# Loading and converting the first layer's weights later in an mLSTM + Fourier-mix kernel

## The chip, the cores and the metric

The kernel runs on one core of one Trainium2 chip. The metric is the device time of one execution in microseconds; lower is better. The time before is the median of six runs.

## The reference

The work is two layers, one behind the other. The first is an mLSTM cell over 4 batches, 8 heads, 768 steps and a head size of 40:

```python
m_new = max(f_t + m, i_t);  fs = exp(f_t + m - m_new);  is_ = exp(i_t - m_new)
C = fs * C + is_ * outer(v_t, k_t);  n = fs * n + is_ * k_t
y_t = sigmoid(o_t) * (C @ q_t) / max(abs(n . q_t), 1)
```

Its output, seen as (4, 768, 320), is x of the second layer, a Fourier mix with an MLP (320 to 1280 to 320):

```python
u = x + real(fft(fft(x, axis=1), axis=2))
un = (u - mean(u)) / sqrt(var(u) + 1e-6)
out = u + relu(un @ w_ch1) @ w_ch2
```

The weights of the MLP come to the kernel as 64-bit floats. The kernel itself makes 32-bit floats of them.

## The kernel before

**Slots.** Every step of the work is a small function, entered into a plan with `at(slot, phase, fn)`. `run` then calls the functions in the order of slot and phase (`EVAC` 0, `FILL` 1, `MAIN` 2, `FILL_PE` 3, with fractions between), and the instructions of each engine stand in that order in its queue. A slot is no fixed time. What decides is the order alone: an engine takes its instructions one by one, and each waits by semaphores for what it needs. All loads are issued by SyncE (SP), in the order of the plan too.

**The first batch.** Batch 0 goes through the mLSTM in six chunks of 128 steps, one every three slots from slot 0 on. For a chunk, ScalarE (ACT) makes the exponentials W (`mlstm_exp`, L491), TensorE (PE) the scores (`mlstm_scores`, L539), VectorE (DVE) weighs them (`mlstm_weigh`, L545), PE makes the products from the state and the chunk (L553, L560, L570, L575), ACT copies the new state and heads out (`mlstm_gather`, L583 to L601), PE turns the heads (`mlstm_turn`, L611), and DVE divides and gates (`mlstm_finish`, L712 to L720). GpSimd (POOL) scales values and states (L507, L530, L501). The Fourier mix of batch 0 folds pairs of chunks at slots 16, 19 and 22 (`mix_fold`, L812 to L830, DVE and POOL), multiplies with the tables (`mix_seq`, `mix_tail`, L901 to L904), adds and takes statistics (`mix_add`, L955 to L963), centres (`mix_center`, uc, L971), turns (L978) and copies out (L983). `halves_of_chunks` (L342, L347 on POOL, among others) prepares the other batches beside it.

**The MLP.** Its first products of batch 0 (`mlp_in`, L1056, and L1047 for the 64 middle features) begin at slot 31, one f of ten for the first half of the tokens in each slot; `mlp_relu` (L1071, ACT) follows. From slot 32 on, the mLSTM of batch 1 runs between them in half chunks (`halves_...`, L515, L519, L652, L667, L672), with a copy of one element on ACT (`halves_between`, "warm", L699) between two groups of PE products.

**The weights.** They come in ten pieces of 128 x 640 numbers, `Piece` (L382): five of w_ch1, then five of w_ch2. Counted from 0, pieces 0 and 3 of w_ch1 are the first and the second half of the columns of rows 0 to 127, pieces 1 and 4 the same of the last 128 rows, and piece 2 is the 64 rows between (`w1t_sb`). A piece has four steps: `load` (L396, 640 KB, SP), `take` (two DVE operations: exponent e, L406, and upper mantissa m, L408), `convert` (two ACT operations, L413 and L414) and `join` (three DVE operations, L420, L422 and L426; the last writes the weights). Two `raw` buffers take turns, so the load of piece n waits until piece n - 2 is joined; of e and m there is one buffer each.

Product f of `mlp_in` uses the second half of the columns (pieces 3 and 4) from f = 4 and f = 5 on, at slots 35 and 36; piece 2 is first used at f = 1.

Of the kernel before, what the change touches and what calls it, by code (L numbers as in the profile page):

```python
# [53 lines left out]
def kernel(  # L54
# [87 lines left out]
    def gates(gp):  # L142
# [40 lines left out]
        w1_pieces[0].load()  # L183
        nc.sync.dma_start(out=spread_sb, in_=spread)
        mlstm_load(0, 2)
        w1_pieces[1].load()
        for t in hT_bufs + Cd_bufs + [h_first]:
            nc.gpsimd.memset(t, 0.0)

# [192 lines left out]
    class Piece:  # L382
# [33 lines left out]
        def join(self):  # L416
# [7 lines left out]
            for d in self.dst:  # L424
# [5 lines left out]
    w1_pieces = [Piece([w1_sb[:, f // 2, f % 2 * part:(f % 2 + 1) * part]], w_ch1[:, f * part:(f + 1) * part])  # L430
                 for f in (0, 2, 1, 3)]
# [16 lines left out]
    def mlstm_load(b, c):  # L448
        k = chunks[b, c] = Chunk()
        i = b * NT + c  # L450
        k.qk = qk_bufs[i % NQ]
        k.C = [C_bufs[(i + n) % 3] if b == 0 else states[(b * NS + 2 * c + n) % len(states)] for n in range(3)]
        for hip in range(2):
            nc.sync.dma_start(out=k.qk[hip * 64:hip * 64 + D], in_=qkT[b, c, hip])
        kvt = kvp.tile([L, H * (D + D1) + LH - D], FP, name="kvt", tag="kvt")
        nc.sync.dma_start(out=kvt, in_=kv[b, c])
        k.v, k.k = kvt, kvt[:, H * D1:]
        k.v1 = k.v[:, 0:H * D1].rearrange("p (h d) -> p h d", d=D1)
        k.kn = k.k[:, 0:H * D].rearrange("p (h d) -> p h d", d=D)
# [844 lines left out]
    ctx.enter_context(tc.manual_schedule())  # L1304
    gates_pool = ExitStack()
    gates(gates_pool.enter_context(tc.tile_pool(name="gates", bufs=1)))


# [31 lines left out]

    at(60, FILL + 0.4, lambda: nc.gpsimd.memset(ds_sb[0:1, 0, 0, :], 1.0))

    when = [((2, 0.7), (4, 0.5), (6, 0.6)), ((6, 0.7), (7, 0.5), (8, 0.6)), ((11, 0.7), (13, 0.5), (22, 0.6))]
    when += [((22, 0.7), (23, 0.7), (31, 0.5)), ((31, 0.7), (32, 0.7), (33, 0.6))]
    when += [((s, 0.7), (s + 1, 0.7), (s + 2, 0.6)) for s in (36, 39, 42, 48, 51)]
    pieces = w1_pieces + w2_pieces
    for n, (w, p) in enumerate(zip(when, pieces)):
        if n > 4:
            at(when[n - 2][2][0] + 1, FILL + 0.7, p.load)
        for (s, phase), fn in zip(w, (p.take, p.convert, p.join)):  # L1350
            at(s, FILL + phase, fn)

    early = [(3, mlstm_load, 3), (3, mlstm_load_o, 2), (4, mlstm_load, 4), (5, mlstm_load_decay, 3),
             (5, mlstm_load_decay, 4), (6, None, 2), (7, mlstm_load_o, 3), (7, mlstm_load, 5),
             (11, mlstm_load_decay, 5), (11, None, 3), (11, mlstm_load_o, 4), (12, load_tables, None),
             (14, mlstm_load_o, 5), (23, None, 4)]
    for s, load, c in early:
        at(s, FILL + 0.8, *((pieces[c].load,) if load is None else (load,) if c is None else (load, 0, c)))

# [127 lines left out]
```

## Time and profile before

| | us |
|---|---|
| median of 6 runs | 396.47 |
| lowest, highest | 395.22, 396.68 |
| time of the profiled execution | 396.68 |
| its span, first to last instruction | 395.0 |

| stretch, us | what runs | DVE busy | ACT busy | POOL busy | DMA engines busy |
|---|---|---|---|---|---|
| 10 to 15 | first chunks of batch 0 | 3.49 | 3.96 | 4.53 | 1.03 |
| 25 to 30 | chunks | 4.61 | 4.39 | 2.79 | 0.94 |
| 40 to 45 | last chunk, first folds | 4.66 | 3.00 | 2.34 | 0.47 |
| 50 to 55 | mix of batch 0 | 4.13 | 2.90 | 0.00 | 1.02 |
| 65 to 70 | first MLP products, batch 1 begins | 3.52 | 3.71 | 3.41 | 1.05 |
| 75 to 80 | the same | 4.66 | 2.72 | 1.16 | 0.55 |

Busy times are microseconds out of the five of each stretch; the share of the DMA engines is 1 when all 16 are busy. The granted clock of TensorE is 1.00 throughout. The slots can be read in the trace from their operations: the first load of a piece is issued at 4.54 us, the takes of the ten pieces start at 14.1, 22.3, 31.5, 52.3, 61.9, 79.0, 86.8, 94.6, 109.0 and 117.1 us, and the first MLP product starts at 59.55 us.

In lines of the timeline, the columns are the start (us from the start of the span), the busy time (us), the engine, the source line, the operation, the tile written and those read, shapes and count; a bracket holds the idle time of the engine before it and what ended that. Lines of the chain of waits have the start, the time and what the chain ran through.

### The profile page before, as it was taken

To read this page: it belongs to the slowest core of one execution; us is meant where nothing else is said; L and a number is where in the kernel's file an instruction comes from. 1 tells how busy PE (TensorE), PEld (TensorE's weight loads), DVE (VectorE), ACT (ScalarE), POOL (GpSimd) and SP (SyncE) were. 2 spreads that over 40 slices of the span, in tenths; PEclk is the share of its full clock that TensorE was granted. 3 is DMA by queue.
4 is the path that set the end of the run, shared out by engine and by line. 5 is a ranking of instruction groups with operands and counts; after the bars stand their busy time and mean duration, and the time that the engine had idled before them with its cause. 6 is when DMAs were issued, how large, how long until landed. Compare 5 with 4: busy or idle time off the path is not lost.

```text
span 395.0 us, 10580 instructions
## 1 busy us (share of the span) xinstructions
PE 380.1 (96%) x4174; PEld 277.1 (70%) x4174; DVE 278.6 (71%) x671; ACT 172.1 (44%) x481; POOL 134.5 (34%) x237
## 2 busy tenths in 40 slices
PE   8999899999999999998999989989999899999996
PEld 6878555556566677664579978755588896556996
DVE  7789988599599677566975598767655785336652
ACT  6887357477443124653462314554530123454000
POOL 5749514377944423271354133541400000020000
PEclk9999999999999999999999999999999999999999
DMA  7988499667692445539400627400000010000000
GB/s 213 295 232 224 153 239 246 193 206 224 190 233 73 145 97 157 147 87 223 121 15 32 157 56 198 146 20 2 0 2 33 0 36 33 2 0 0 35 33 35
DMA packets 25631, 44.78 MB, mean 113 GB/s; under 512 B 5727, under 2 KB 14766, under 8 KB 25454
## 3 DMA queue, kind: packets, MB, share of 16 engines
q1 hardware_dynamic: 25582, 44.11, 40.2%
q8 instruction: 33, 0.54, 0.6%
q14 instruction: 16, 0.13, 0.1%
HBM read 38.49 MB, written 4.12 MB: 108 GB/s over the span
## 4 chain that ended last, share of the span: by engine, by line
PE 75%; DVE 16%; issue 3%; ACT 3%; DMA 1%; POOL 1%; SPq 0%; DVEq 0%; ACTq 0%; POOLq 0%
PE po L1237 18%; PE pm L1118 14%; PE po L1181 8%; PE pm L1056 6%; PE ph L519 4%; PE pm L1123 3%; PE pu L935 3%; PE ps L519 3%; PE pm L1047 2%; PE put L978 2%; PE pz L904 1%; PE pz L892 1%; DVE so L716 1%; DVE h L1127 1%; DVE x L1187 1%
## 5 line engine op out<-in xcount | busy, mean ns | idle before, releaser
L1187 DVE SCALAR_TENSOR_TENSOR x<-po,rstd,x 128x160 f32<-128x160 f32 (+1 forms) x69 | 26.9, 394 | 40.9 <-PE po L1237 36.8
L1127 DVE TENSOR_TENSOR h<-h,pm 128x384 f32<-128x384 f32 x60 | 30.5, 549 | 29.0 <-PE pm L1123 13.8
L1118 PE MATMUL pm<-uT,w_sb 128*128 128x384 f32 x90 | 37.7, 506 | 2.1 <-DVE h L1127 1.3
L652 POOL TENSOR_TENSOR C<-C,decB 128x164 f32<-128x164 f32 x30 | 15.9, 531 | 69.5 <-DVE C L667 53.0
L491 ACT ACTIVATE W<-W,colT 128x64 f32<-128x64 f32 x144 | 37.5, 339 | 0.0
L1181 PE MATMUL po<-w_sb,h 128*128 128x320 f32 x120 | 34.3, 435 | 0.0
L515 POOL TENSOR_SCALAR_AFFINE_SELECT W<-W 64x512 f32<-64x512 f32 x36 | 27.3, 758 | 12.9 <-ACT W L491 11.4
L1002 POOL TENSOR_TENSOR t<-rstd 128x6 f32<-128x6 f32 x12 | 3.3, 274 | 80.7 <-DVE v L996 80.2
L1237 PE MATMUL po<-T,S 128*128 128x160 f32 x180 | 27.9, 302 | 1.5 <-DVE x L1187 1.5
L1056 PE MATMUL pm<-uT,w_sb 128*128 128x384 f32 x80 | 29.2, 500 | 0.1
L1181 PEld LDWEIGHTS po<-w_sb,h 128*128 128x128 f32 x120 | 22.2, 190 | 9.6 <-issue 0.6
L501 POOL TENSOR_TENSOR qg<-qk,Gb 128x512 f32<-128x512 f32 (+1 forms) x21 | 27.4, 1305 | 1.2 <-DMA Gb<-G_d 1.2
L1237 PEld LDWEIGHTS po<-T,S 128*128 128x128 f32 x180 | 25.5, 190 | 3.2 <-DVE x L1187 2.0
L1118 PEld LDWEIGHTS pm<-uT,w_sb 128*128 128x128 f32 x90 | 15.5, 189 | 16.4 <-DVE h L1127 7.5
L1237 PE MATMUL po<-w_sb,h 128*128 128x160 f32 x180 | 26.3, 300 | 0.0
L1237 PEld LDWEIGHTS po<-w_sb,h 128*128 128x128 f32 x180 | 25.2, 190 | 1.4 <-DVE x L1187 0.3
L1174 ACT ACTIVATE h<-h 128x384 f32<-128x384 f32 x45 | 23.1, 520 | 2.0 <-DVE h L1127 2.0
L507 POOL TENSOR_TENSOR vw<-kvt,colT 128x328 f32<-128x328 f32 x23 | 19.4, 845 | 13.1 <-DMA qk<-in_qkT 10.1
L983 ACT COPY uT<-put 128x384 f32<-128x384 f32 x24 | 11.1, 477 | 29.0 <-PE put L978 29.0
L1123 PE MATMUL pm<-uT,w1t_sb 64*128 64x384 f32 x120 | 23.4, 508 | 0.0
L971 ACT ACTIVATE uc<-x 128x384 f32<-128x384 f32 x24 | 14.4, 613 | 17.9 <-DVE x L963 11.9
L1056 PEld LDWEIGHTS pm<-uT,w_sb 128*128 128x128 f32 x80 | 14.1, 189 | 9.6 <-issue 1.9
(241 smaller groups left out, 843.7 us busy)
## 6 DMA issues: line engine op xcount, KB each, us to landing
kvt<-in_kv SPq DMA_DIRECT2D x24, 336.0 KB
qk<-in_qkT SPq DMA_DIRECT2D x48, 160.0 KB
raw<-in_w SPq DMA_DIRECT2D x10, 640.0 KB
Gb<-G_d SPq DMA_DIRECT2D x36, 128.0 KB
W<-M_d SPq DMA_DIRECT2D x36, 128.0 KB
so<-in_o SPq DMA_DIRECT2D x24, 160.0 KB
out<-x SPq DMA_DIRECT2D x24, 160.0 KB
x<-so SPq DMA_DIRECT2D x9, 140.0 KB
```

The lines of the kernel that those rows point to most:

```text
L491: nc.scalar.activation(out=k.W[:, h, :], in_=M, func=AF.Exp, scale=-1.0, bias=colT[:, c, 0, b * H + h:b * H + h + 1])
L501: nc.gpsimd.tensor_tensor(out=k.qg[:, :, t], in0=k.qk[:, 0, :, t], in1=k.Gb[:, :, t], op=OP.mult)
L515: nc.gpsimd.affine_select(out=W, in_=W, compare_op=OP.is_ge, fill=0.0, base=base, pattern=[[0, H], [step, LH]], channel_multiplier=-1)
L519: nc.tensor.matmul(out, w, x, start=start, stop=True, skip_group_check=True)
L1056: nc.tensor.matmul(k.pm[i], w1_sb[:, ch, f0:f0 + L], u[2 * ch], start=(ch == 0 and not ahead), stop=(ch == 1 and ahead), skip_group_check= ...
L1118: nc.tensor.matmul(bank, w, u, start=start, stop=True, skip_group_check=True)
L1123: nc.tensor.matmul(bank, block(w1t_sb, i)[rows], mlp_u(gr, 1)[rows], start=False, stop=True, skip_group_check=True)
L1127: nc.vector.tensor_tensor(out=h, in0=h, in1=bank, op=OP.add)
L1174: nc.scalar.activation(out=h, in_=h, func=AF.Relu, scale=-1.0)
L1181: nc.tensor.matmul(k.po[gr, i], hidden(gr, f)[:, i * L:(i + 1) * L], w2_sb[:, f, :], start=(f == 0), stop=(f == NFF - 1))
L1187: nc.vector.scalar_tensor_tensor(out=u, in0=po, scalar=k.rstd[:, c:c + 1], in1=u, op0=OP.mult, op1=OP.add)
L1237: nc.tensor.matmul(po, a[:, f], w[:, f], start=start and f == 0, stop=f == half - 1, skip_group_check=True)
```

## The change

The numbers of `when` and `early`, and one line in `gates`, are altered; no operation is added or left out. Slots of take, convert and join, and of the load:

| piece | take | convert | join | load, before | take | convert | join | load, after |
|---|---|---|---|---|---|---|---|---|
| 0 | 2 | 4 | 6 | ahead of slot 0 | 5 | 7 | 8 | ahead of slot 0 |
| 1 | 6 | 7 | 8 | ahead of slot 0 | 19 | 20 | 22 | 8 |
| 2 | 11 | 13 | 22 | 6 | 22 | 23 | 31 | 13 |
| 3 | 22 | 23 | 31 | 11 | 31 | 32 | 33 | 23 |
| 4 | 31 | 32 | 33 | 23 | 33 | 34 | 35 | 31 |

The loads of the first two pieces of w_ch2 go by the slots of the joins of pieces 3 and 4, plus one: slots 34 and 36 in place of 32 and 34. In slot 31 the load of piece 4 stands where that of the first piece of w_ch2 stood in the queue of SP.

```diff
@@ gates
         mlstm_load(0, 2)
-        w1_pieces[1].load()
@@
-    when = [((2, 0.7), (4, 0.5), (6, 0.6)), ((6, 0.7), (7, 0.5), (8, 0.6)), ((11, 0.7), (13, 0.5), (22, 0.6))]
-    when += [((22, 0.7), (23, 0.7), (31, 0.5)), ((31, 0.7), (32, 0.7), (33, 0.6))]
+    when = [((5, 0.7), (7, 0.5), (8, 0.6)), ((19, 0.7), (20, 0.7), (22, 0.6)), ((22, 0.7), (23, 0.7), (31, 0.5))]
+    when += [((31, 0.7), (32, 0.3), (33, 0.6)), ((33, 0.65), (34, 0.1), (35, -0.1))]
@@
     early = [(3, mlstm_load, 3), (3, mlstm_load_o, 2), (4, mlstm_load, 4), (5, mlstm_load_decay, 3),
-             (5, mlstm_load_decay, 4), (6, None, 2), (7, mlstm_load_o, 3), (7, mlstm_load, 5),
-             (11, mlstm_load_decay, 5), (11, None, 3), (11, mlstm_load_o, 4), (12, load_tables, None),
-             (14, mlstm_load_o, 5), (23, None, 4)]
+             (5, mlstm_load_decay, 4), (8, None, 1), (7, mlstm_load_o, 3), (7, mlstm_load, 5),
+             (11, mlstm_load_decay, 5), (13, None, 2), (11, mlstm_load_o, 4), (12, load_tables, None),
+             (14, mlstm_load_o, 5), (23, None, 3), (31, None, 4)]
```

The numbers in `when` are added to `FILL`, so that (19, 0.7) stands after the fold of slot 19 (`FILL + 0.5`) and ahead of `mlstm_finish` of chunk 5 (slot 21), and the join at (35, -0.1) stands just ahead of the `mix_add` of slot 35.

## The prediction

> **What bounds the kernel now.** I read the page first: its shares of busy time.
>
> ```profile
> PE 380.1 (96%) x4174; PEld 277.1 (70%) x4174; DVE 278.6 (71%) x671; ACT 172.1 (44%) x481; POOL 134.5 (34%) x237
> ```
>
> TensorE is busy 96% of the span, so a change gains what it takes out of TensorE's gaps and loses what it puts into them. Second, the timeline of PE from 12 to 130 us, for every instruction that starts after a gap over 0.2 us (the bracket is the gap and what ended it):
>
> ```profile
> 16.64 0.44 PE L299 MATMUL pd<-dec,spread_sb 32*128 32x80 f32 x2 [0.43 <-DVE dec L295]
> 24.26 0.66 PE L611 MATMUL px<-ident,h 128*128 128x128 f32 x4 [0.40 <-ACT h L601]
> ...
> 36.94 0.63 PE L611 MATMUL px<-ident,h 128*128 128x128 f32 x4 [0.27 <-DVE den L712]
> ...
> 48.03 0.92 PE L904 MATMUL pz<-ds_sb,fe 128*128 128x385 f32 x2 [0.23 <-POOL fe L819]
> ...
> 82.48 0.44 PE L519 MATMUL ph<-kvt,W 64*64 64x41 f32 x16 [0.50 <-ACT warm L699]
> ```
>
> The others are 29.88 (0.40, ACT h), 40.87 (0.82, ACT C), 44.18 (0.74, ACT h), 55.82 (0.35, ACT uc); from 59.55 to 82.48 there is none. Only two are ended by VectorE, the engine that loses work early. Third, the chain of waits of the same stretch does run through conversions:
>
> ```profile
> 14.09 0.76 DVE e L406
> 14.86 0.94 DVE m L408
> ...
> 24.57 0.73 ACT e L413
> 25.32 0.82 DVE e L420
> ...
> 31.60 0.96 DVE e L406
> ```
>
> A chain names one way back; that TensorE was busy all along beside it shows that it is worth no more than those gaps. Fourth, the timeline of DVE where work arrives:
>
> ```profile
> 45.08 1.18 DVE L815 COPY fe<-eo 128x2 f32<-128x2 f32 x1
> ...
> 67.65 0.68 DVE L672 TENSOR_TENSOR W<-ps,W 128x512 f32<-128x512 f32 x1
> 68.25 0.31 DVE L667 TENSOR_TENSOR C<-C,ps 128x164 f32<-128x164 f32 x1
> 70.77 0.49 DVE L955 TENSOR_TENSOR x<-x,pu 128x320 f32<-128x320 f32 x1 [2.21 <-PE pu L935]
> ...
> 74.64 0.33 DVE L667 TENSOR_TENSOR C<-C,ps 128x164 f32<-128x164 f32 x1 [2.64 <-PE ps L519]
> ...
> 78.96 0.48 DVE L406 TENSOR_SCALAR e<-raw 128x640 uint32<-128x640 uint32 x1
> 80.34 0.96 DVE L420 SCALAR_TENSOR_TENSOR e<-raw,e 128x640 uint32<-128x640 uint32 x1 [0.26 <-ACT e L413]
> 81.22 1.89 DVE L422 SCALAR_TENSOR_TENSOR m<-raw,m 128x640 f32<-128x640 uint32 x1
> ```
>
> The only room is 2.21 + 2.64 us at 68.6 to 74.6; from 74.64 to 98.5 VectorE has hardly a pause.
>
> **What the Trainium skill says.** "SBUF — State Buffer", section "Who interferes with whom": VectorE and GpSimd share a port pair; a VectorE operation in a two-port mode, or with two SBUF inputs against a GpSimd operation that reads SBUF, excludes GpSimd and is excluded by it, for a whole instruction. The trace agrees: L406 and L408 take 0.48 us each beside an idle POOL, 1.04 and 1.57 at 31.5 us, where POOL works without a pause, and a copy of two columns (L815) took 1.18 us behind three POOL operations. "TensorE: Matmul & The Clock Gate", section "Architectural detail": VectorE and ScalarE run strictly in order; so one late operation holds back all behind it, as in each list above.
>
> **The change, part by part.** A piece costs: take (L406, L408) 0.97 us clean, up to 2.5 when POOL interferes; convert (L413, L414, ACT) 0.83 + 0.72 = 1.5; join (L420, L422, L426) 2.4 clean (49.82 to 52.23), 4.0 against POOL (80.34 to 84.30).
>
> *(1) Less before slot 19.* Two takes, two converts and a join leave. TensorE gains at two gaps. At 16.64 it waits for dec, which without the take would still wait for the decays (ACT L247, 14.81 + 1.26 = 16.07); dec starts at 16.1 in place of 16.32: 0.25. At 36.94 the transposes wait for a bank until finish of chunk 1 has read it, and finish stood behind the take of 31.5 to 34.0: all 0.27. The gaps of ACT stay: its converts stood after the copies that TensorE waits for. Gain 0.5.
>
> *(2) Loads.* SP issues the same ten loads of 640 KB. The one at 8.23 goes to slot 8 (about 26 us), that of 22.91 behind the tables (36.6), that of 29.38 to the place of 51.40, that of 51.40 to the place of 62.81; w2's first goes from 62.81 to the place of 66.48, its second from there behind the W loads of 74.86. No chain link up to 82 us is a DMA, so emptier queues at 8 to 35 us gain nothing. The w2 loads land within about 4 us, before their takes at 79 and 87; behind the second stand so and Gb of slot 37 (76.41, 77.09), whose users come at 88 to 90. Nothing, while those covers hold.
>
> *(3) Piece 1 at slots 19 to 22.* Its take stands between the second and the third fold, ahead of finish of chunk 5, at 46.4. VectorE gets there earlier: with finish of chunk 3 done sooner, the two-column copy L815 falls before the POOL operations that blocked it, which saves up to 1.0, and (1) gives 0.5. The take costs 1.0 to 2.5 there, POOL being busy from 45.0 to 48.0. Finish then starts 0.5 earlier to 1.0 later than before; the fold ends at 49.8 now, some 0.5 before TensorE needs it. TensorE: 0.5 earlier to 0.6 later; I take 0.2 later, (1) included. The convert falls in ACT's idle time 45.3 to 50.6. The join takes the place of the old third one, and slots 22 to 33 have one piece for another: nothing. w1t's join now ends at 61.81, 0.5 before L1047 at 62.33; both follow the same chain, so they move together.
>
> *(4) The fifth piece, the cost that decides.* In slots 33 to 35 a whole piece is added, and its raw data are loaded at the old place of 62.81. The packets of the load issued there ended at 68.7, by the trace's DMA records; VectorE would be ready at 67.7. So: take 68.75 to 69.65; behind it W and L667 to 70.45 (68.55 before); join from 70.55, against L652 and L501 on POOL, 3.6 (between 2.4 and 4.0), to 74.2. Behind it stands the addition of slot 35 (L955, at 70.77 before) with its statistics, 1.2, to 75.4; then L667, L949, L950, L955 and statistics to 77.5, where finish began at 76.74. The two idle stretches are used up and VectorE is 0.7 late. It meets L406 at 78.96: from there L413 (79.47), L491, uc and the copy L699 (82.30) run straight on in ACT to TensorE's gap at 82.48. Lateness becomes time: 0.7, and 0.2 more as the load of 51.40 waits for a join that (3) delays. On ACT the convert makes the relus of 68.30 wait to about 72.0; TensorE wants their bank at 72.1. The first product on the new weights is at 74.67, half a us after the join. Bounds of (4): 0.4 below zero (clean join, data at 67.7, all idle time used) to 2.
>
> The two effects on TensorE, 0.2 from (3) and 0.9 from (4), don't add: the second is a time before which VectorE isn't there. Everything after 84 us keeps its order and moves along. Sum: profiled execution 396.68 (span 395.0 and 1.7 around it) + 0.9 = 397.6. That execution is 0.2 above the median of the runs, 396.47; so **397.4**.
>
> **Rivals.** *Hidden (not slower).* The idle 4.85 us hold the added 0.97 + 2.4 = 3.4 plus up to 1.4 us of waiting. The point is whether take and join of the fifth piece, waits included, end before 73.5: with the data there by 68.2 and one POOL collision, they do, and the gain of (1) remains: 0.3 to 0.7 less (0.25 + 0.27 + 0.23 at 48.03), about 396.0. For it: VectorE's idle time is real, and the DMA queues run ahead by (1). Against: POOL works from 64.9 to 71.7 with few breaks. Chance 0.28.
> *Data later.* If the raw data of piece 4 land at 70 to 70.5, as DMA engines are busy 0.91 to 1.05 of the time from 50 to 70 us, VectorE and ACT stand still with relus behind them, TensorE waits for the bank at 72 and for the weights at 74.7: 2.0 to 2.4 more, about 398.6. Against: the queue ahead of that load is the old one. Chance 0.12.
> *The fold.* The take before finish of chunk 5 is shut out by POOL for its full 2.5: TensorE 0.6 to 1.0 later at 50 us, and (4) adds nothing to that: 397.2. Chance 0.15.
> The forecast has 0.45. That the loads and conversions don't move as said is excluded: the order is written out by slot.
>
> **The numbers.** About 0.2% (0.8 us) can be told from no change here. Slower by more: 0.34 of the forecast's 0.45, all of the late data's 0.12, half of the fold's 0.15: 0.54. Faster by more: 0.11 of the hidden case's 0.28. The rest, 0.35. The range goes from the hidden case with all three gaps gone, 395.7, to the late data, 398.9. The likeliest case's own is 396.9 to 397.9.
>
> **What would show it.** (1): no gap at 36.9, that at 16.6 down to 0.2, and no third one gone. (3): the take of piece 1 between 1.0 and 2.5 us long, gap before pz under 0.6. (4): the take after 67.7 starts with a wait for the load; L955 of slot 35 ends near 74.7 in place of 71.3; the gap ended by warm L699 grows from 0.5 to over 1 us. The forecast is wrong if that gap has not grown, or if TensorE loses time in a stretch after 85 us that the order of before does not explain.

## The result, and the profile after

The changed kernel is slower: 399.01 us in the median of 19 runs (397.10 to 402.89) beside 396.39 us of the kernel before (40 runs, 395.22 to 400.99). One more run of the changed kernel, of 403.95 us, was in a slow state and is not counted. The ratio is 1.0074, with a 95% interval of 1.0055 to 1.0092. That is 2.6 us more, where 0.9 had been forecast; it lies just outside the range.

The profiled execution has a span of 400.0 us (401.68 in all), 5.0 more than before, and is one of the longer runs. Source lines behind L186 have numbers lower by one than before. The timeline of PE after, the starts that answer to the five shown of before, as far as they are still there:

```profile
16.43 0.44 PE L298 MATMUL pd<-dec,spread_sb 32*128 32x80 f32 x2 [0.21 <-DVE dec L294]
24.05 0.66 PE L610 MATMUL px<-ident,h 128*128 128x128 f32 x4 [0.40 <-ACT h L600]
...
48.49 0.92 PE L903 MATMUL pz<-ds_sb,fe 128*128 128x385 f32 x2 [1.23 <-POOL fe L818]
...
74.65 1.29 PE L1055 MATMUL pm<-uT,w_sb 128*128 128x384 f32 x2 [1.96 <-ACT h L1070]
```

The gap of 0.43 has halved, and that of 36.94 is gone, as forecast. The gap before pz, a product of the mix with the tables, has grown from 0.23 to 1.23, and there is a new one of 1.96 us at 74.65, where the third product of f = 4 waits for a bank that a relu (L1070) has to read first. The gap at 82.48 is no longer there.

What stood ahead of that relu, in the timeline of ACT after:

```profile
44.66 0.47 ACT L604 ACTIVATE so<-so 128x320 f32<-128x320 f32 x1 [1.06 <-DMA so<-in_o]
45.04 0.51 ACT L332 ACTIVATE x<-w_sb 32x384 f32<-32x384 f32 x1
...
71.81 0.83 ACT L412 ACTIVATE e<-e,ebias 128x640 uint32<-128x640 uint32 x1 [4.05 <-DVE e L405]
72.55 0.72 ACT L413 ACTIVATE m<-m 128x640 f32<-128x640 uint32 x1
73.17 1.05 ACT L490 ACTIVATE W<-W,colT 128x64 f32<-128x64 f32 x4
74.12 0.84 ACT L1070 ACTIVATE h<-pm 128x384 f32<-128x384 f32 x2
```

and what the conversion waited for, in the timeline of DVE after:

```profile
66.95 1.24 DVE L425 TENSOR_TENSOR w_sb<-m,e 128x640 f32<-128x640 f32 x1
71.28 0.49 DVE L405 TENSOR_SCALAR e<-raw 128x640 uint32<-128x640 uint32 x1 [3.09 <-DMA raw<-in_w]
```

VectorE stood still for 3.09 us for the raw data of piece 4, ACT behind it, the relus behind that, TensorE last. The ACT lines show a second wait for a load, of 1.06 us: so (the data of the output gate) of chunk 5, behind which ACT makes the two operations (L332, L333) that POOL's fold stands behind. These are the same stretches by windows (busy us of PE, PEld, DVE, ACT, POOL, then the granted clock of TensorE, the share of the DMA engines and GB/s):

```profile
70.00:75.00 5.00, 3.04 (x12) 1.27 (x11) 3.69 (x7) 3.19 (x9) 1.91 (x2) 1.00 0.77 232
75.00:80.00 5.00, 5.00 (x116) 3.72 (x114) 3.59 (x8) 1.95 (x7) 3.16 (x5) 0.50 0.04 10
80.00:85.00 5.00, 5.00 (x17) 2.23 (x15) 4.14 (x12) 2.28 (x8) 1.12 (x3) 0.81 0.66 201
```

Behind its gap TensorE ran at half the clock, for 6.8 us by the clock's own record (75.05 to 81.87; the lines give the same: 5 us, and 0.19 x 5 / 0.5 = 1.9 in the last stretch). The 5.0 us of this execution are so made up: the first MLP product starts at 60.02 (0.47 late); the gap is 1.96; from the product that ends it to the products of f = 6 pass 7.87 us (74.65 to 82.52), where before, counted from 72.22, the end of the product ahead, it was 4.53, so 3.3 more, about half of the 6.8 us; and the old gap of 0.50 is saved. That gives 5.2.

The clock explains a good part of the spread of the runs. Of the 19, eleven had a mean clock of 1.00, with a median of 398.56; four had 0.996 (398.77 to 402.89) and four 0.991 (401.61 to 402.28). All of 146 runs of the kernel before beside the experiments had 1.00 or 0.999. So about 2.2 us belong to the waits and half a us of the median to the clock.

### The profile page after: what moved, and what is told of

It reads as the page before. It is cut to its first block, busy times and chain, and to the rows that moved or that the text cites. A ratio compares the mean times of both kernels' runs of the same rounds, so it can differ in the third digit from the quotient of the medians.

```text
span 400.0 us, 10581 instructions
## 1 busy us (share of the span) xinstructions
PE 383.1 (96%) x4174; PEld 278.8 (70%) x4174; DVE 277.5 (69%) x671; ACT 172.1 (43%) x481; POOL 133.7 (33%) x237
## 4 chain that ended last, share of the span: by engine, by line
PE 73%; DVE 14%; ACT 3%; DMA 3%; issue 3%; SPq 1%; POOL 1%; DVEq 0%; POOLq 0%; ACTq 0%
PE po L1236 18%; PE pm L1117 14%; PE po L1180 8%; PE pm L1055 6%; PE ph L518 4%; PE pm L1122 4%; PE ps L518 3%; PE pu L934 3%; DMA so<-in_o 2%; PE pm L1046 2%; DVE h L1126 2%; PE put L977 2%; PE pz L903 1%; PE pz L891 1%; DVE x L1186 1%
## 5 line engine op out<-in xcount | busy, mean ns | idle before, releaser
L1117 PE MATMUL pm<-uT,w_sb 128*128 128x384 f32 x90 | 37.7, 506 | 2.0 <-DVE h L1126 1.3
L1055 PE MATMUL pm<-uT,w_sb 128*128 128x384 f32 x80 | 30.6, 517 | 2.1 <-ACT h L1070 2.0
```

The lines of the kernel that those rows point to most:

```text
L1055: nc.tensor.matmul(k.pm[i], w1_sb[:, ch, f0:f0 + L], u[2 * ch], start=(ch == 0 and not ahead), stop=(ch == 1 and ahead), skip_group_check= ...
L1117: nc.tensor.matmul(bank, w, u, start=start, stop=True, skip_group_check=True)
```

## The experiments

Every kernel is compared with runs of the kernel before on the same chip. Where an edit adds lines, source lines behind them have numbers higher by up to three. Theory 1 said that the places of two loads make the loss; its rival was the prediction's own account, the added work on VectorE and its collisions with POOL.

**The load of piece 2 behind so of chunk 5.** In the queue of SP, the change had put it in front.

```diff
-             (13, None, 2), ... (14, mlstm_load_o, 5), (23, None, 3), (31, None, 4)]
+             ... (14, mlstm_load_o, 5), (14, None, 2), (23, None, 3), (31, None, 4)]
```

> The kernel after, with the load of piece 2 moved from slot 13 to behind the load of so of chunk 5 in slot 14. Theory 1 (order of the loads): in the profile after, ACT waited 1.06 us for this so and TensorE 1.2 us for the fold at 48.5 us behind it; here the gap before pz goes to 0.2 to 0.3, the first MLP product comes at 59.0 to 59.2 in place of 60.0, and the time falls by 0.5 to 1.0 us. The later stall at 72 to 75 us stays. Theory 2 (the take of piece 1 beside POOL is the price): the gap before pz stays over 0.8 and the time is that of after.

397.29 us, 1.0026 (1.0015 to 1.0037). The wait for so went, but TensorE's gap before pz didn't: it was 1.30, now ended by DVE. Theory 1 was half wrong here: another price appeared at the same place. The time fell for another reason: in its profile VectorE waited 0.71 us for piece 4, not 3.09, and TensorE had no gap at 75. Why these data came earlier there isn't shown.

**Piece 4's conversion behind the relus.**

```diff
-((33, 0.65), (34, 0.1), (35, -0.1))
+((33, 0.65), (35, -0.95), (35, -0.1))
```

> The kernel after, with the two ACT operations of piece 4's conversion moved from slot 34 to just behind the relus of slot 35. The wait of VectorE for the raw data stays. Theory 1: TensorE's gap of 1.96 us came from the relus queued behind the conversion on ACT, so it goes; TensorE then waits for the weights of piece 4 themselves (f = 5, about 75 us in time after) for 0 to 1.5 us, and the granted clock stays at 1.00 more often; the time falls by 1 to 2 us. Theory 2 (VectorE's lateness of the prediction alone, ACT no part): the gap stays or comes back in full at f = 5 and the time is within 0.5 us of after.

398.75 us, 1.0057 (1.0035 to 1.0078), not told from after. The gap only moved, to the first product on the new weights (timeline of PE):

```profile
77.88 1.27 PE L1055 MATMUL pm<-uT,w_sb 128*128 128x384 f32 x2 [1.85 <-DVE w_sb L425]
```

So the order on ACT decides where TensorE stops, and putting it right is not enough: with a wait of 3.66 us for the data in this execution, 0.6 longer than in the profile after, the weights themselves were late.

**Piece 4 loaded in slot 25.** Both raw buffers are taken then, so its data go into a hidden buffer of the MLP that is still unused.

```diff
+            if self is w1_pieces[4]:
+                self.raw = hid[1, 0][:, 0:2 * n].bitcast(mybir.dt.int64)
+            else:
                 self.raw = cp.tile(...)
-             (23, None, 3), (31, None, 4)]
+             (23, None, 3), (25, None, 4)]
```

> The kernel after, with the raw data of piece 4 loaded in slot 25 in place of 31, into the still unused hidden buffer of the MLP (no raw buffer is free earlier). Theory 1: the wait of 3.1 us on VectorE goes, TensorE's gap at 74.7 with it, the clock is 1.00 in all runs; 0.5 to 0.7 us of TensorE's gap at 48.5 stay in the time, so 396.8 to 397.3. Theory 2 (the added take, convert and join alone use up VectorE's idle time): the gap at 82.5 is 1 us or more and the time stays over 398.

396.90 us, 1.0018 (1.0010 to 1.0027). One load takes 2.0 of the 2.6 us away. The gap at 75 is gone, and that behind the copy "warm" is as before the change; the gap before pz stays (PE):

```profile
48.42 0.91 PE L906 MATMUL pz<-ds_sb,fe 128*128 128x385 f32 x2 [1.16 <-POOL fe L821]
...
82.88 0.44 PE L521 MATMUL ph<-kvt,W 64*64 64x41 f32 x16 [0.50 <-ACT warm L701]
```

**Both loads moved.**

> Both: piece 2's load behind so of chunk 5, and piece 4's load in slot 25 into the unused hidden buffer. Theory 1: nothing is left but the relief of VectorE before slot 19, 0.5 us, and what the gap at 82.5 gives or takes; 395.6 to 396.4, at or a little under the kernel before. Theory 2: over 397.

397.26 us, 1.0020 (1.0013 to 1.0028): no better than the one load alone. Theory 1 missed; theory 2 has the time, and the gap before pz is still there, now ended by DVE. The timelines of DVE and PE show what took the place of the wait for so:

```profile
44.36 1.21 DVE L817 COPY fe<-eo 128x2 f32<-128x2 f32 x1
...
45.72 1.03 DVE L408 TENSOR_SCALAR e<-raw 128x640 uint32<-128x640 uint32 x1
46.67 0.81 DVE L410 TENSOR_SCALAR m<-raw 128x640 uint32<-128x640 uint32 x1
```
```profile
50.20 1.67 PE L906 MATMUL pz<-ds_sb,fe 128*128 128x385 f32 x4 [1.30 <-DVE fe L821]
```

With so in time, POOL's copies come earlier and shut out the two-column copy (1.21 us in place of 0.17) and the take of piece 1, which needs 1.7 us, and finish of chunk 5 and the last fold come late. With so late, as in the profile after, POOL was late, and the same copy took 0.17 and the take 0.9. The two prices stand side by side and either costs TensorE about 1 us.

**The take of piece 1 in slot 11**, with both loads moved, and with piece 4's alone.

```diff
-((19, 0.7), (20, 0.7), (22, 0.6))
+((11, 0.7), (13, 0.5), (22, 0.6))
```

> The kernel with both loads moved (piece 2's behind so of chunk 5, piece 4's in slot 25 into the unused hidden buffer), and the take and the convert of piece 1 in slots 11 and 13 in place of 19 and 20. Theory A: once so comes in time, what holds the last fold is the take of piece 1 on VectorE between the folds (1.7 us beside POOL in the run with both loads); so TensorE's gap of 1.3 us before pz goes, and the time falls by 0.8 to 1.3 us to 395.7 to 396.4. The gap of 0.27 at 36.9 us of before may come back. Theory B: the gap before pz has another cause, stays at 1 us or more, and the time stays at 397.2.

396.52 us, 1.0026 (1.0006 to 1.0045). The gap before pz is 0.23 again, so theory A is right on that; the next wait stood ready, though, since the change loads piece 1 in slot 8 only (DVE, then PE, in a profiled execution of 397.86 us, one of the longer ones):

```profile
32.62 0.62 DVE L408 TENSOR_SCALAR e<-raw 128x640 uint32<-128x640 uint32 x1 [1.70 <-DMA raw<-in_w]
```
```profile
37.29 0.63 PE L613 MATMUL px<-ident,h 128*128 128x128 f32 x4 [1.19 <-DVE den L714]
```

> The same take and convert in slots 11 and 13, piece 4's load in slot 25, but piece 2's load left in slot 13 ahead of so of chunk 5. Theory A (two prices side by side, the later one decides): ACT still waits about 1 us for so, POOL's fold comes late, and TensorE's gap before pz is 0.8 to 1.2, now ended by POOL; the time stays at 396.7 to 397.0. Theory B (the take alone is the price): the gap goes and the time is that of the kernel with all three moved.

396.93 us, 1.0016 (1.0009 to 1.0024), the time of theory A without its mechanism: in this execution VectorE waited 2.65 us for piece 1, and TensorE took 1.4 us more than before from one product to another (22.65 to 43.94; before, 24.26 to 44.18); ACT then came late enough not to wait for so, and the gap before pz was 0.23.

**Piece 1 loaded ahead of slot 0 as well.**

```diff
         mlstm_load(0, 2)
+        w1_pieces[1].load()
```

> The kernel with both loads moved and the take and convert of piece 1 in slots 11 and 13, and now also its load ahead of slot 0, as before: in the run with the load in slot 8, VectorE waited 1.7 us for it in slot 11 and TensorE 1.2 us behind. Theory A: this wait was all that was left; the gap at 37 us falls to 0.3, that at 16 us stays at 0.2, and the time is 0.1 to 0.4 us under the kernel before (395.8 to 396.1). Theory B: the relief of VectorE before slot 19 is worth nothing by itself, or the early data of piece 1 delay other loads: 396.3 or more.

396.16 us, 0.9998 (0.9989 to 1.0006). With all three loads in time the loss is gone (gaps 0.21 at 16, 0.26 at 36, 0.24 before pz). The expected gain is too small for the interval.

**The late half alone**, once with piece 4's data early and once as in the change. Pieces 0 and 1 are those of the kernel before.

```diff
-    when = [..., ((11, 0.7), (13, 0.5), (22, 0.6))]
-    when += [((22, 0.7), (23, 0.7), (31, 0.5)), ((31, 0.7), (32, 0.7), (33, 0.6))]
+    when = [..., ((22, 0.7), (23, 0.7), (31, 0.5))]
+    when += [((31, 0.7), (32, 0.3), (33, 0.6)), ((33, 0.65), (34, 0.1), (35, -0.1))]
-             ... (11, None, 3), ... (23, None, 4)]
+             ... (23, None, 3), (25 or 31, None, 4)]
```

> The late half of the change alone: pieces 0 and 1 as in the kernel before, pieces 2, 3 and 4 in the slots of the kernel after, with piece 4's data loaded in slot 25 into the unused hidden buffer. Theory A: a whole piece of conversion between the first MLP products and the batch 1 chunks costs nothing if its data are there; no take stands between the folds; the gap of 0.27 at 36.9 goes. 395.9 to 396.4, the time of before. Theory B (the prediction's own step: take and join use up VectorE's idle time and the gap at 82.5 grows): 0.7 us more, 397.0.

396.16 us, 0.9994 (0.9988 to 1.0000). A whole piece of conversion at 67 to 72 us costs nothing. Its lines in the timeline of DVE, and the gap behind in PE:

```profile
67.09 0.50 DVE L409 TENSOR_SCALAR e<-h 128x640 uint32<-128x640 uint32 x1
67.50 0.49 DVE L411 TENSOR_SCALAR m<-h 128x640 uint32<-128x640 uint32 x1
...
68.73 0.82 DVE L423 SCALAR_TENSOR_TENSOR e<-h,e 128x640 uint32<-128x640 uint32 x1
...
73.97 0.33 DVE L670 TENSOR_TENSOR C<-C,ps 128x164 f32<-128x164 f32 x1 [0.46 <-PE ps L522]
```
```profile
81.83 0.44 PE L522 MATMUL ph<-kvt,W 64*64 64x41 f32 x16 [0.51 <-ACT warm L702]
```

The two idle stretches of before (2.21 and 2.64) hold all of it, and 0.46 us of them is left.

> The same late half, but with the data of piece 4 loaded in slot 31, as in the kernel after. Theory A: this one load makes most of the change's loss: VectorE waits 1 to 4 us for it, TensorE loses 0 to 2 us at 72 to 76 us and in a part of the runs the granted clock is under 1.00; median 397.2 to 399. Theory B: the loss needs the early half too (so, take between the folds): within 0.5 us of the late half with the early load.

397.95 us, 1.0035 (1.0021 to 1.0048), 395.9 to 400.75: theory A. It is the same kernel but for one load, with its buffer (DVE, then PE):

```profile
70.29 0.49 DVE L406 TENSOR_SCALAR e<-raw 128x640 uint32<-128x640 uint32 x1 [3.13 <-DMA raw<-in_w]
```
```profile
73.66 0.91 PE L1056 MATMUL pm<-uT,w_sb 128*128 128x384 f32 x2 [2.00 <-ACT h L1071]
```

**A gap without the change.** This is the kernel before, with ACT held up ahead of the relus of slot 35 by ten or eight copies into an unused buffer.

```diff
+    def hold_act(n):
+        for _ in range(n):
+            nc.scalar.copy(out=out, in_=rest.unsqueeze(1).to_broadcast([L, 2, 2 * L]))
+    at(35, -0.5, hold_act, 10 or 8)
```

> The kernel before, with ten copies of 128 x 512 (about 5.5 us of ACT) ahead of the relus of slot 35 into an unused buffer; no load and no piece is moved. TensorE has 3.3 us of room there before it misses the bank, so it should stand still for about 2.0 to 2.3 us near 72 us. Theory A: a gap of 2 us of TensorE costs more than itself in a part of the runs, because the granted clock halves for some 4 us after it, as in the profile after: 1.7 us in the runs at clock 1.00 (2.2 less the gap of 0.5 at 82.5), about 4 in the others, median 398 to 400. Theory B: the halved clock has to do with the change (its DMA, its DVE work), not with the gap: all runs at 1.00 and 398.1.

401.49 us, 1.0134 (1.0102 to 1.0166). In the profiled execution the gap was 2.83 (more than expected), the clock 1.00 and the time 398.55; the other five runs had clocks of 0.987 to 0.996 and 400.66 to 403.38.

> The same with eight copies (about 4.4 us): a gap of 1.0 to 1.2 us. Theory A: short enough for the clock to stay at 1.00; 0.6 us more than before, 396.9 to 397.1. Theory B: the same time; a clock under 1.00 in a part of the runs would say that even this gap is long enough.

397.81 us, 1.0047 (1.0034 to 1.0061), clock 1.00 or 0.999 in all five. The gap was 1.53, more than expected here too. The gaps of the two profiled executions, with ten copies and then with eight:

```profile
73.94 0.91 PE L1056 MATMUL pm<-uT,w_sb 128*128 128x384 f32 x2 [2.83 <-ACT h L1071]
```
```profile
72.75 0.91 PE L1056 MATMUL pm<-uT,w_sb 128*128 128x384 f32 x2 [1.53 <-ACT h L1071]
```

No load or conversion was moved here, so the halved clock needs nothing of the change: a gap of TensorE is enough. The 4 us of half clock that were expected are not what the records show: 6.8 us in the profile after, 3.4 with the conversion behind the relus.

**The late half, with the take of piece 0 out of the way of the decay.**

```diff
-    when = [((2, 0.7), (4, 0.5), (6, 0.6)), ...
+    when = [((4, 0.6), (4, 0.7), (6, 0.6)), ...
```

> The late half with the early load of piece 4, and the take of piece 0 moved from slot 2 to slot 4, behind the two operations that the state's decay needs. Theory A (TensorE's gaps are all that early relief is worth): the gap at 16.3 us falls from 0.42 to 0.2, that at 36.9 stays gone, so 0.2 us less than the late half alone and 0.4 less than the kernel before: 395.8 to 396.0. Theory B: the take now delays the copy of the decay (L303) and the weighing behind it, another gap opens before 24 us, and the time is 396.2 or more.

395.82 us, 0.9986 (0.9978 to 0.9994): faster than both kernels, by about as much as the two early gaps hold (0.22 + 0.27). In its profiled execution (396.41, one of the longest of 22) the gap at 36.9 is gone and that at 16 is down, but ACT waited 0.50 us for so and the gap before pz was 0.67, so that this one execution shows no gain (ACT, then PE):

```profile
43.85 0.47 ACT L608 ACTIVATE so<-so 128x320 f32<-128x320 f32 x1 [0.50 <-DMA so<-in_o]
```
```profile
16.17 0.44 PE L299 MATMUL pd<-dec,spread_sb 32*128 32x80 f32 x2 [0.21 <-DVE dec L295]
...
47.68 0.92 PE L907 MATMUL pz<-ds_sb,fe 128*128 128x385 f32 x2 [0.67 <-POOL fe L822]
```

## Why the prediction was wrong

Its direction was right and its size was not: 2.6 us for 0.9. Two terms failed above all: the wait for the data of the fifth piece, put at 1.0 us and measured at 3.09, and the clock, put at nothing. The path was another one too. The forecast led the loss through VectorE to the gap at 82 us, which was to grow to over 1 us; by its own sign it was wrong, for that gap is gone. The loss came at 74.65, through the relus behind the conversion on ACT, for which the forecast had left 0.1 us (72.0 for 72.1).

*(1), less before slot 19*: right. The gaps were 0.21 and none, dec started at 16.10 as said, and the median of the last kernel is lower by about as much.

*(2), the loads*: wrong. "No chain link up to 82 us is a DMA" described the old order; I asked of each load when its own data would be used and not, for those ahead of slot 31, which load it was put in front of. Piece 2's 640 KB came before so of chunk 5: 1.06 us of ACT. Moving the load away removed the wait and not the gap, since the take took over. That the wait alone makes the gap can be read from the last kernel, which has no take between the folds: 0.50 of wait and a gap of 0.67 in place of 0.23. There piece 2's load does not stand right in front of so, so that so can be late without it too; how much of the 1.06 us is the new order's is open.

*(3), the take between the folds*: the collision with POOL was there, 1.7 us in the runs where so came in time, within the bounds of 1.0 to 2.5. I counted L815 as saved; it was so only where POOL was late, as in the profile after. TensorE was 0.47 late at the first MLP product there (0.2 forecast, 0.6 the bound). By comparison of the early-load kernel (0.6 over before) with the late half (0.2 under), the early half costs about 0.8 us.

*(4), the fifth piece*: the term mis-sized is the wait for its data. I took the last data packet of the load issued at 62.81, at 68.7, where by the DMA records the 128th packet of its size ended. But the next load's packets have the same size and lie among them: by 70.12 there had ended 153, where one load has 128. What the operation waits for is that all sixteen DMA engines report, and by the semaphore records the last of them did so at 70.12 before the change, 0.8 after the fifteenth; after it, at 71.19, 1.5 after the fifteenth. "DMA: Bandwidth & Descriptors" of the Trainium skill, section "Why a DMA increments its semaphore by 16 and not by 1", says that the engines finish independently and only the full sixteen means landed; the trace agrees: VectorE started at 71.28, just behind the sixteenth. The wait was 3.09 us in place of 1.0: 1.4 from that reading (70.12 for 68.7) and 1.1 from the load's later landing (71.19), less 0.5 by which VectorE came later itself. The rest of the step stood: a join of 3.6 us was forecast and 3.6 measured (68.73 to 72.37 in the late half), with no lateness at 82 us once the data are there. The rival "data later" had the mechanism, the bank at 72 included, at a chance of 0.12; it set its landing at 70 to 70.5. That its 398.6 is the median of the runs at clock 1.00 (398.56) is luck in part, as it has neither the clock nor the early half's cost.

*The clock* was in no case. Every gap had been counted at its own length.

*Hidden*, the rival on the other side, is what the late half with the early load does: its condition, take and join done before 73.5, is met at 72.4.

Open: why the sixteenth engine trails, and by a different amount in each run; and how much of the difference between eight of 19 runs of the change with a lowered clock and one of seven of the late half comes from the place of the gap (below) and how much from gaps of other lengths, since only one run of each was profiled. A few runs of kernels whose profiled gaps were under 1.3 us (3 of 18 with the take in slot 11 and both loads moved, 2 of 22 with piece 4's load alone) had a lower clock too; whether their gaps were longer isn't known.

## What to carry to other kernels

When work is moved later, its load usually moves too: ask when the load can be issued (here, when a buffer comes free), read the landing from the moment its last DMA engine reports, and look at which loads it now stands in front of. The conversion itself was free in idle time; the waits in front of it were not. A wait for one engine becomes one for all whose work stands behind it in order, and a saved wait is worth no more than the distance to the next one.

## What the runs showed of the hardware

A gap of some 2 us in TensorE can cost more than twice itself, since its clock can fall to one half behind it. In the profile after this was 3.3 us on top of 1.96. With eight copies (gap 1.53 in the profiled execution) the clock stayed in five of five runs, and with ten (2.83) it was lowered in five of six. "TensorE: Matmul & The Clock Gate" of the Trainium skill, section "HAM oscillation — how this bites in real kernels", gives idle gaps of more than about 3.4 us as what to avoid; here 1.96 us was enough, and the measurement decides.

The length alone does not decide. While TensorE works, the clock's record changes only after whole multiples of 3.41 us: in the profile after, 68.27 us at full clock are twenty of them, 6.83 at half two, 317.44 at full 93; with the conversion behind the relus, half the clock lasted 3.41. Laid out in such stretches, the gaps of the profiled executions fall into two groups. Those that lie within one stretch (1.96 in the profile after, 2.00 in the late half with the late load, 1.85 with the conversion behind the relus) were each followed by half the clock from the stretch's end on; in the profile after the gap is at 72.69 to 74.65, the stretch at 71.64 to 75.05. Those that a stretch's end cuts (2.83 into 1.42 and 1.41 with ten copies, 1.53 into 1.22 and 0.31 with eight, and 1.99 into 0.4 and 1.6 before pz with the conversion behind the relus) left it at 1.00. So what counts seems to be TensorE's idle time within one stretch, with the limit here between 1.6 and 1.85 us; six gaps say so, and no run was made to test it. It would explain why the same kernel keeps its clock in one run and loses it in the next. A mean clock of 0.996 or 0.991 is then one or two stretches at half (an estimate: half of 3.41 us is 0.0043 of 397).

Three POOL operations in a row shut out one small VectorE copy for all three (1.11 to 1.21 us in place of 0.17, in five profiles): in the profile with both loads moved the copy started with the first of them, at 44.36, and ended at 45.57, just behind the third (45.54), so it was not let in between them.
